# Attention with a token mixer: v instead of k times cos and sin, q transposed once, stacked k'v tiles, whole-tile stores and a new order

## The chip, the cores and the metric

One core of a Trainium2 chip. The metric is the device time of one execution in microseconds (us), compared as medians and as means over fast runs. A run counts as slow when it is more than 1.5% above the fastest run of the same kernel. Profiles show one execution; its span is about 1.8 us shorter than its time. The *granted clock* is the share of its full clock that TensorE was allowed. An *evacuation* is a copy of a result out of PSUM, the memory into which TensorE writes; a store has *landed* when its last byte has arrived.

## The reference, cut to what matters

```python
# q, k, v: (batch 8, heads 8, seq 576, dim 64) fp32; result (8, 576, 512) fp32
def phi(x, c, s):
    r = np.maximum(x, 0.0)
    return np.concatenate([r * c, r * s], axis=-1)      # 64 -> 128 features
q_p, k_p = phi(q, cos_w, sin_w), phi(k, cos_w, sin_w)   # angle = pi/2 * pos / 576
kv  = np.einsum('bhsf,bhsd->bhfd', k_p, v)
z   = np.sum(k_p, axis=2)
num = np.einsum('bhsf,bhfd->bhsd', q_p, kv)
den = np.einsum('bhsf,bhf->bhs', q_p, z)[..., None] + 1e-06
x   = num / den                                  # heads side by side: (8, 576, 512)
wq, wk = x @ w_q, x @ w_k                        # 512 -> 64
W_tok  = 1/8 * np.einsum('bsd,btd->bst', wq, wk)
out    = np.maximum(np.einsum('bst,btd->bsd', W_tok, x), 0.0) @ w_out
```

## The kernel before

The whole kernel is a list of words such as `MK.3.0@V`: an operation, its indices, and the engine (V VectorE, A ScalarE, G GpSimd, T TensorE with a PSUM bank, Y SyncE's DMA queue). Each engine executes its words in the order of the list. A *double pair* `H` is four heads of one batch. A *pair* `g` is two heads, which lie on the 128 partitions as 2 x 64 rows of 9 positions each. There are 16 double pairs and 32 pairs.

For each pair VectorE made two products of 1152 elements (`MK`: relu(k) times cos and sin; `EQ`: transposed q times cos and sin), one cast of k'v out of PSUM (`EK`), a denominator and its reciprocal (`RC`), and one normalisation (`XN`).

```python
def MK(eng, pb, H, s):                       # k' = relu(k) * (cos, sin), line L232
    eng.tensor_mul(kp[H % N_KP][:, lo:hi],
        rk[H % N_RK][:, lo:hi].unsqueeze(3).to_broadcast([P, n, C9, 2, D]),
        cossin.unsqueeze(1).to_broadcast([P, n, C9, 2, D]))

def DQ(eng, pb, H, s):                       # relu(q), written twice (QREP = 2)
    relu(eng, qd[H % N_QD][:, lo:hi]..., raw["q"]...to_broadcast([P, n * C9, QREP, D]))

def QK(eng, pb, g):                          # per pair: 18 products and 18 transposes
    for c in range(C9):
        for hh in range(2):
            p0 = hh * 64
            T.matmul(kvp[:, hh, :], kp[H % N_KP][p0:p0 + 64, i, c, :, :],       # L260
                     vb[H % N_VB][p0:p0 + 64, i, c, 0:D + 1], ...)
    ... # 18 transposes of the doubled q, 64 x 128 each (L269)

def NM(eng, pb, g):                          # 10 products over 128 rows, L292
    for hh in range(2):
        for u in range(SC):
            T.matmul(nv[:, hh, u, :], qpt[g % N_QPT][:, hh, 2 * u:2 * u + 2, :],
                     kvs[g % N_KV][:, hh, :], ...)

def RC(eng, pb, g):
    eng.tensor_scalar_add(rec[g % 4], den, EPS)
    eng.reciprocal(rec[g % 4], rec[g % 4])

# ... XT: 20 transposes of 64 rows per double pair; WQK, TK, KX, MX: the mixer

def WO(eng, pb, b, t):                       # one output tile: 4 products, L413
    for dmc in range(NDM):
        T.matmul(o, mix[...][:, dmc, base:base + P], wo_sb[:, dmc, :],
                 start=(dmc == 0), stop=(dmc == NDM - 1))

def ST(eng, pb, b, u, hi):                   # half a tile: 64 partitions
    dst = dataclasses.replace(out, offset=out.offset + row * DM,
        ap=[[C9 * DM, 64], [2 * DM, len(ts)], [1, DM]])
    eng.dma_start(dst, osb[n % N_OSB][64 * hi:64 * hi + 64, 0:len(ts), :])
```

Of the kernel before, what the change touches and what calls it, by code (L numbers as in the profile page):

```python
# [24 lines left out]
N_RAW, N_RK, N_KP, N_QD, N_VB, N_QPT, N_KV = 4, 2, 3, 3, 3, 4, 4  # L25
N_XS, N_XT, N_WQK, N_WKJ, N_KX, N_MIX, N_OSB = 3, 2, 2, 2, 2, 2, 6
QREP = 2
EPS_PE = False
LD_PAIR = True
SPLIT = (0, 1, 2, 3, 4, 5, 6, 7, 8, 9, 10, 11, 12, 13, 14, 15)  # L30
# [7 lines left out]
LD.k.1.0@Y LD.k.0.0@Y LD.v.0.0@Y LD.k.0.1@Y LD.q.1.1@Y LD.q.0.1@Y LD.q.0.0@Y LD.k.1.1@Y  # L38
LD.v.0.1@Y RK.1.0@V MK.1.0@V RK.0.0@V LD.v.1.1@Y LD.v.1.0@Y CV.0.0@V RK.0.1@A LD.q.2.1@Y
MK.0.0@V LD.q.1.0@Y MK.0.1@V LD.k.2.0@Y DQ.0.0@G LD.k.2.1@Y LD.v.2.1@Y RK.1.1@V DQ.0.1@G QK.0@T0  # L40
CV.0.1@A LD.v.2.0@Y EQ.0@V DQ.1.1@G QK.1@T2 CV.1.1@A LD.q.3.0@Y EK.0@V MK.1.1@V NM.0@T0 CV.1.0@A
LD.q.2.0@Y EQ.1@V QK.3@T4 DQ.2.1@G LD.v.3.0@Y RC.0@V EK.1@V LD.k.3.1@Y EQ.3@V DQ.1.0@G EK.3@V
LD.k.3.0@Y RK.2.0@A XN.0@V NM.3@T2 QK.2@T4 LD.v.3.1@Y RK.2.1@A MK.2.0@V MK.2.1@V CV.2.1@A
LD.k.4.0@Y RC.3@V QK.5@T0 CV.2.0@A LD.k.5.1@Y EQ.2@V NM.1@T6 EK.2@V DQ.3.0@G LD.q.3.1@Y XN.3@V
NM.2@T4 LW.qk@Y EK.5@V DQ.2.0@G RC.2@V RC.1@V LD.v.5.1@Y XN.2@V CV.3.0@G EQ.5@V LD.q.5.1@Y
XT.1@T2 XN.1@V LD.q.5.0@Y RK.3.0@A NM.5@T0 QK.4@T4 RK.3.1@A MK.3.0@V LD.k.5.0@Y XT.0@T6 CV.3.1@A
MK.3.1@V EX.1@A LD.v.4.0@Y EQ.4@V LD.q.4.0@Y EK.4@V RK.5.1@A RC.5@V QK.6@T2 LD.v.5.0@Y EX.0@A
NM.4@T4 EK.6@V CW.qk@G LD.q.4.1@Y RC.4@V RK.4.0@A MK.5.1@V WQK.0@T6 LD.k.4.1@Y CV.5.1@A DQ.3.1@G
XN.4@V LD.v.4.1@Y XN.5@V EW.0@A DQ.5.1@G LW.o@Y EQ.6@V DW.0@A XT.2@T0 TK.0@T4 LD.k.6.0@Y
MK.4.0@V QK.7@T6 EX.2@A QK.11@T2 EWK.0@V CV.4.0@G LD.k.6.1@Y EK.7@V EQ.7@V NM.6@T4 RK.5.0@G  # L50
LD.q.6.0@Y KX.0@T0 RC.6@V DQ.5.0@G XN.6@V NM.7@T6 LD.v.6.0@Y EKX.0@A CV.5.0@A DQ.4.0@G MX.0.2@T0
RC.7@V LD.k.7.0@Y MX.0.3@T4 EQ.11@V EMX.0.3@A EK.11@V LD.q.6.1@Y EMX.0.2@A MK.5.0@V MX.0.0@T4
MX.0.1@T2 RK.4.1@A QK.8@T0 LD.v.7.0@Y CV.4.1@G XN.7@V EMX.0.0@A DQ.4.1@G EQ.8@V EMX.0.1@A
XT.3@T6 QK.10@T4 EK.8@V EX.3@A MK.4.1@V NM.8@T0 EQ.10@V QK.9@T2 CW.o.0@G CW.o.1@A LD.v.6.1@Y
EK.10@V WQK.1@T6 EQ.9@V LD.q.7.0@Y RK.6.0@G EK.9@V NM.10@T4 RC.8@V LD.k.7.1@Y EW.1@A MK.6.0@V
WO.0.2@T2 LD.k.8.1@Y DQ.6.0@G RC.10@V NM.9@T6 XN.8@V EO.0.2@A WO.0.1@T3 LD.v.8.0@Y RK.6.1@A
XN.10@V CV.6.0@G TK.1@T2 EO.0.1@A LD.v.7.1@Y RK.7.0@G RC.9@V QK.12@T0 EWK.1@A XN.9@V DQ.6.1@G
LD.q.7.1@Y NM.11@T4 WO.0.0@T2 RC.11@V LD.k.8.0@Y MK.6.1@V KX.1@T3 EO.0.0@A LD.q.8.0@Y MK.7.0@V
DW.1@A WO.0.3@T6 CV.6.1@G EQ.12@V LD.k.9.0@Y EKX.1@A CV.7.0@A DQ.7.0@G MX.1.1@T2 EK.12@V
LD.v.10.0@Y XN.11@V EO.0.3@A QK.13@T0 EMX.1.1@A RK.7.1@G MX.1.0@T6 LD.k.9.1@Y QK.14@T4 EQ.13@V  # L60
EMX.1.0@A RK.8.1@G XT.4@T2 LD.v.8.1@Y EK.13@V EK.14@V MX.1.2@T6 MK.7.1@V WO.1.1@T0 EMX.1.2@A
LD.q.9.0@Y MK.8.1@V EX.4@A NM.12@T6 LD.q.8.1@Y WO.1.2@T1 DQ.7.1@G EQ.14@V EO.1.1@A LD.q.9.1@Y
RC.12@V XT.5@T2 CV.7.1@A RK.8.0@G XN.12@V NM.13@T4 LD.v.9.0@Y EX.5@A WO.1.0@T0 CV.8.0@G RC.13@V
DQ.8.0@G LD.k.10.1@Y XN.13@V MX.1.3@T6 RK.9.0@A QK.15@T2 LD.k.10.0@Y MK.8.0@V EO.1.2@A WQK.2@T4
EO.1.0@A MK.9.0@V LD.q.10.0@Y EMX.1.3@A CV.10.0@G EQ.15@V NM.14@T0 LD.v.9.1@Y EW.2@A QK.16@T6
RK.9.1@G RC.14@V CV.8.1@A EK.15@V LD.q.10.1@Y TK.2@T4 XN.14@V NM.15@T2 EWK.2@A WO.1.3@T5 DW.2@A
DQ.8.1@G LD.k.12.0@Y EQ.16@V EK.16@V LD.q.11.1@Y XT.6@T0 RC.15@V DQ.9.1@G QK.17@T6 EX.6@A
XN.15@V LD.k.11.1@Y KX.2@T4 CV.9.0@G EQ.17@V XT.7@T2 RK.10.1@G EKX.2@A EK.17@V EO.1.3@A EX.7@V
DQ.9.0@G MX.2.1@T0 NM.17@T6 EMX.2.1@A MX.2.0@T4 RC.17@V WQK.3@T2 EMX.2.0@A MK.9.1@V RK.10.0@A
CV.9.1@G XN.17@V MX.2.2@T0 QK.18@T4 EW.3@A LD.k.14.0@Y MK.10.1@V WO.1.4@T6 EMX.2.2@A ST.1.0.0@Y  # L70
MK.10.0@V LD.v.11.1@Y MX.2.3@T0 QK.19@T2 DW.3@G EQ.18@V ST.1.1.1@Y EMX.2.3@A TK.3@T7 DQ.10.0@G
EK.18@V ST.0.0.0@Y EK.19@V EWK.3@A NM.16@T0 EQ.19@V EO.1.4@A NM.18@T4 ST.1.0.1@Y WO.2.1@T7
DQ.10.1@G RC.16@V RC.18@V LD.k.11.0@Y XN.16@V QK.20@T2 ST.0.0.1@Y EO.2.1@A DQ.11.1@G XN.18@V
RK.12.0@A LD.v.10.1@Y KX.3@T0 RK.11.1@A CV.11.1@G LD.q.11.0@Y EQ.20@V NM.19@T4 EKX.3@A
LD.v.11.0@Y XT.8@T6 EK.20@V RC.19@V MX.3.1@T0 ST.0.1.0@Y EX.8@A MK.12.0@V WO.2.0@T2 LD.v.12.0@Y
XN.19@V RK.11.0@G WO.2.3@T3 LD.k.12.1@Y EMX.3.1@A MK.11.1@V ST.1.1.0@Y EO.2.0@A MX.3.2@T4
XT.9@T0 MK.11.0@V LD.v.12.1@Y QK.23@T6 EO.2.3@A LD.q.12.0@Y CV.10.1@G EX.9@V EMX.3.2@A NM.20@T2
ST.0.1.1@A DQ.11.0@G EK.23@V MX.3.3@T4 EQ.23@V WQK.4@T0 CV.11.0@A LD.q.13.1@Y RC.20@V EMX.3.3@A
LD.q.12.1@Y XN.20@V QK.22@T6 EW.4@A QK.21@T4 LD.k.13.0@Y EQ.22@V TK.4@T0 MX.3.0@T2 EK.21@V
RK.12.1@G ST.1.2.1@A WO.2.2@T1 EK.22@V EQ.21@V EWK.4@A LD.k.13.1@Y NM.23@T6 EMX.3.0@A MK.12.1@V  # L80
NM.22@T4 LD.v.13.1@Y EO.2.2@A KX.4@T0 RC.23@V RK.14.0@G CV.12.0@A XN.23@V NM.21@T2 ST.1.2.0@Y
DQ.12.0@G EKX.4@A WO.3.3@T1 RC.22@V LD.q.13.0@Y RC.21@V CV.12.1@G XN.22@V WO.3.0@T0 EO.3.3@A
LD.v.13.0@Y XN.21@V DW.4@A XT.11@T4 DQ.12.1@G ST.2.0.0@Y QK.24@T6 EX.11@V MX.4.2@T2 LD.q.14.0@Y
WO.3.2@T1 EMX.4.2@A EQ.24@V RK.13.0@G EO.3.0@A LD.v.14.0@Y EK.24@V MX.4.0@T2 MK.14.0@V QK.25@T4
EMX.4.0@A LD.k.15.0@Y MX.4.3@T6 RK.13.1@G WO.3.1@T0 EK.25@V EO.3.2@A EQ.25@V DQ.13.1@G
LD.k.14.1@Y EMX.4.3@V XT.10@T2 EO.3.1@A ST.2.0.1@Y MX.4.1@T4 WO.3.4@T1 MK.13.0@V EMX.4.1@A
ST.3.1.0@Y MK.13.1@V NM.24@T6 EO.3.4@A WO.4.0@T0 LD.v.15.0@Y CV.13.0@G RC.24@V EX.10@A XN.24@V
DQ.13.0@G NM.25@T4 LD.q.15.0@Y WO.4.1@T1 RC.25@V EO.4.0@A LD.k.15.1@Y CV.13.1@G XN.25@V QK.26@T2
EO.4.1@A DQ.14.0@G LD.q.14.1@Y QK.27@T6 CV.14.0@A EQ.26@V XT.12@T0 LD.v.14.1@Y RK.15.0@A
QK.28@T4 EK.26@V EK.27@V EX.12@A EQ.27@V RK.14.1@G ST.3.2.1@Y WQK.5@T2 EK.28@V LD.q.15.1@Y  # L90
MK.14.1@V WO.4.2@T6 EW.5@A MK.15.0@V ST.2.1.0@Y NM.27@T0 DW.5@G EQ.28@V EO.4.2@A NM.26@T2
TK.5@T7 CV.15.0@G RC.27@V EWK.5@A NM.28@T4 RC.26@V DQ.15.0@G WO.4.3@T6 XN.27@V RK.15.1@A RC.28@V
KX.5@T7 XN.26@V EO.4.3@A DQ.14.1@G QK.30@T0 EKX.5@A ST.4.1.1@Y XN.28@V MX.5.3@T2 MX.5.1@T6
LD.v.15.1@Y CV.14.1@G EQ.30@V EMX.5.3@A XT.13@T4 ST.4.1.0@Y EMX.5.1@A EK.30@V QK.29@T2 EX.13@V
ST.3.0.1@Y ST.2.1.1@A DQ.15.1@G MX.5.0@T0 NM.30@T6 EK.29@V ST.3.0.0@Y EMX.5.0@A EQ.29@V WQK.6@T4
ST.4.0.1@Y ST.3.1.1@A RC.30@V MK.15.1@V WO.5.0@T0 ST.3.2.0@Y EW.6@A XN.30@V CV.15.1@G ST.4.0.0@Y
NM.29@T2 DW.6@G TK.6@T1 RC.29@V MX.5.2@T4 QK.31@T6 EWK.6@V EMX.5.2@A XN.29@V KX.6@T1 EO.5.0@A
EK.31@V WO.5.4@T4 EQ.31@V ST.5.0.0@Y EKX.6@V NM.31@T2 ST.5.0.1@Y MX.6.0@T0 RC.31@V MX.6.1@T6
EMX.6.0@A WO.5.2@T5 XN.31@V EO.5.4@A EMX.6.1@V XT.14@T0 EO.5.2@A XT.15@T2 WO.5.3@T4 EX.14@V
EX.15@V WO.6.0@T5 EO.5.3@A WQK.7@T0 ST.5.2.0@A ST.5.2.1@Y EO.6.0@V WO.6.1@T2 EW.7@V MX.6.3@T4  # L100
DW.7@G MX.6.2@T0 EO.6.1@A TK.7@T3 EMX.6.2@V WO.5.1@T6 EWK.7@A ST.6.0.1@Y EMX.6.3@A ST.6.0.0@A
KX.7@T7 EO.5.1@V WO.6.3@T0 EKX.7@V ST.5.1.0@A ST.5.1.1@Y MX.7.1@T2 MX.7.3@T4 MX.7.0@T6 EMX.7.1@A
WO.6.2@T1 EMX.7.0@V EO.6.3@A EMX.7.3@V MX.7.2@T2 EO.6.2@A WO.7.1@T6 EMX.7.2@A ST.6.1.0@Y
WO.7.2@T7 ST.6.1.1@A EO.7.1@V WO.7.4@T0 EO.7.2@A WO.7.3@T1 ST.7.1.0@Y ST.7.1.1@A EO.7.4@V
WO.7.0@T2 ST.7.3.0@A EO.7.3@V ST.7.3.1@A ST.7.2.0@Y EO.7.0@A ST.7.2.1@Y ST.7.0.0@A ST.7.0.1@Y
"""


@with_exitstack
def kernel(  # L110
    ctx: ExitStack,
    tc: tile.TileContext,
    q: bass.AP,
    k: bass.AP,
    v: bass.AP,
# [83 lines left out]

    def part(H, s):  # L200
        return (s, s + 1) if H in SPLIT else (0, 2)

    def LD(eng, pb, t, H, s):
        lo, hi = part(H, s)
        b, h = divmod(H, 2)
# [48 lines left out]
    def QK(eng, pb, g):  # L254
# [8 lines left out]
        for c in range(C9):  # L263
            for hh in range(2):
                p0 = hh * 64
                src = qd[H % N_QD][p0:p0 + 64, i, c, :, :]
                if QREP == 1:
                    src = src.to_broadcast([64, 2, D])
# [240 lines left out]
```

## Time and profile before

The median was 130.89 us in three runs (130.32 to 133.51); the profiled run took 130.29 us, with a span of 128.5 us and a granted TensorE clock of 0.91.

The kernel has one long stage in which VectorE works almost without a break, and a tail in which TensorE finishes the mixer and the output product. The window view of the kernel before shows this, from the first cos/sin product on VectorE (4.1 us) to the last normalisation (108.6 us). Its columns are the stretch, its length, the busy time (with instruction counts) of PE, PEld, DVE, ACT and POOL, the granted clock, the DMA share and GB/s:

```profile
4.10:16.00 11.90, 7.07 (x128) 4.46 (x126) 8.47 (x16) 3.81 (x6) 6.12 (x5) 0.74 1.02 366
16.00:40.00 24.00, 19.15 (x519) 15.71 (x519) 21.99 (x48) 15.77 (x23) 15.45 (x16) 0.70 1.06 382
40.00:80.00 40.00, 36.09 (x848) 24.49 (x845) 37.86 (x80) 29.99 (x53) 26.32 (x28) 1.00 0.85 298
80.00:108.60 28.60, 26.85 (x587) 17.25 (x586) 27.51 (x62) 18.75 (x32) 18.42 (x21) 1.00 0.95 326
```

Subtract the DVE column from the length to get VectorE's idle time: 3.4, 2.0, 2.1 and 1.1 us; it is busy for 95.8 of the 104.5 us.

These further lines of the page of the kernel before are needed later: the chain that ended last, shared out by engine, the doubled q on GpSimd, and the half-tile stores.

```profile
DVE 31%; PE 30%; POOL 10%; DMA 8%; SPq 7%; issue 6%; ACT 3%; ACTq 2%; POOLq 0%
...
L195 POOL TENSOR_SCALAR qd<-qf 128x1152 bf16<-128x1152 f32 x32 | 39.1, 1231 | 12.7 <-DMA qf<-in_q_dram 11.6
...
out_dram<-osb SPq DMA_DIRECT2D x21, 256.0 KB, 4.4
out_dram<-osb ACTq DMA_DIRECT2D x9, 256.0 KB, 4.3
out_dram<-osb SPq DMA_DIRECT2D x9, 128.0 KB, 3.4
...
out_dram<-osb ACTq DMA_DIRECT2D x3, 128.0 KB, 4.0
```

The chain runs about equally through VectorE and TensorE, with 9% in the two queues that issue stores and loads (SPq, ACTq). There are 42 store issues, twelve of them on ScalarE's queue.

### The profile page before, as it was taken

How to read it: one execution, taken by the hardware profiler on the slowest of the kernel's cores; microseconds unless marked ns; L12 is line 12 of the kernel's file. 1: busy time of each engine (PE TensorE's matmuls, PEld its weight loads, DVE VectorE, ACT ScalarE, POOL GpSimd, SP SyncE). 2: the span in 40 equal slices, each digit the busy share in tenths (PEclk: the TensorE clock that was granted, in tenths of full speed). 3: DMA queues.
4: the chain of work that ended last, by engine and by line, in shares of the span. 5: the costliest groups of instructions: out<-in, count | busy, mean ns of one | idle time of the engine just before them, and what ended most of it. 6: DMA issues, size and time to landing. Idle time of an engine off the chain costs nothing.

```text
span 128.5 us, 5197 instructions
## 1 busy us (share of the span) xinstructions
PE 105.4 (82%) x2198; PEld 69.4 (54%) x2198; DVE 106.2 (83%) x227; ACT 77.5 (60%) x124; POOL 69.4 (54%) x81
## 2 busy tenths in 40 slices
PE   5935594887879979878999969889999999999900
PEld 2314584847667546566676557364576775543400
DVE  3466999987899999999999896999999998774600
ACT  7125443966396698974976758647977655147110
POOL 7009817098969979995078252389949740020000
PEclk9995558655799999999999999999999999999995
DMA  4999999999999999992068999999998799468793
GB/s 133 276 389 406 391 391 390 331 392 388 389 387 392 391 385 391 390 386 103 5 146 319 303 360 363 340 329 403 384 377 309 176 341 248 107 197 278 186 289 100
DMA packets 20711, 39.40 MB, mean 307 GB/s; under 512 B 3280, under 2 KB 3280, under 8 KB 20688
## 3 DMA queue, kind: packets, MB, share of 16 engines
q1 hardware_dynamic: 19152, 36.32, 81.8%
q10 hardware_dynamic: 1536, 2.75, 6.1%
q8 instruction: 17, 0.28, 0.9%
q14 instruction: 6, 0.05, 0.1%
HBM read 29.62 MB, written 9.44 MB: 304 GB/s over the span
## 4 chain that ended last, share of the span: by engine, by line
DVE 31%; PE 30%; POOL 10%; DMA 8%; SPq 7%; issue 6%; ACT 3%; ACTq 2%; POOLq 0%
DVE kp L232 10%; PE banks L413 10%; DVE xs L309 8%; DVE qpt L279 7%; POOL qd L195 5%; PE banks L260 5%; SPq L208 5%; DMA qf<-in_q_dram 5%; PE banks L269 4%; DMA vf<-in_v_dram 4%; PE banks L292 3%; SPq L430 2%; DVE rec L305 2%; PE banks L343 2%; POOL vb L189 2%
## 5 line engine op out<-in xcount | busy, mean ns | idle before, releaser
L195 POOL TENSOR_SCALAR qd<-qf 128x1152 bf16<-128x1152 f32 x32 | 39.1, 1231 | 12.7 <-DMA qf<-in_q_dram 11.6
L413 PE MATMUL banks<-wo_sb,mix 128*128 128x512 bf16 x144 | 36.0, 380 | 0.0
L232 DVE TENSOR_TENSOR kp<-rk,cossin 128x1152 bf16<-128x1152 bf16 x32 | 29.2, 932 | 1.4 <-POOL rk L195 1.3
L185 ACT COPY osb<-banks 128x512 f32<-128x512 f32 x31 | 18.0, 589 | 12.9 <-PE banks L413 8.2
L309 DVE TENSOR_TENSOR xs<-banks,rec 128x640 bf16<-128x640 f32 x32 | 25.4, 808 | 0.3
L279 DVE TENSOR_TENSOR qpt<-banks,cst 128x1152 bf16<-128x1152 bf16 x32 | 23.9, 746 | 1.1 <-PE banks L269 0.8
L401 ACT ACTIVATE mix<-banks 128x640 bf16<-128x640 f32 (+1 forms) x27 | 17.4, 656 | 8.7 <-PE banks L388 8.1
L260 PE MATMUL banks<-vb,kp 64*128 64x65 bf16 x576 | 16.7, 202 | 3.8 <-DVE kp L232 1.8
L413 PEld LDWEIGHTS <-mix 128*128 128x128 bf16 x144 | 12.1, 98 | 12.5 <-issue 1.4
L292 PE MATMUL banks<-kvs,qpt 128*128 128x65 bf16 x320 | 16.2, 203 | 3.1 <-DVE kvs L187 2.2
L269 PE MATMUL banks<-ident,qd 64*128 64x64 bf16 x576 | 16.2, 201 | 2.2 <-POOL qd L195 2.2
L292 PEld LDWEIGHTS <-qpt 128*128 128x128 bf16 x320 | 13.8, 103 | 7.1 <-DVE qpt L279 2.5
L260 PEld LDWEIGHTS <-kp 64*128 64x128 bf16 x576 | 13.6, 100 | 7.2 <-DVE kp L232 2.5
L193 ACT ACTIVATE rk<-kf 128x576 bf16<-128x576 f32 x15 | 10.1, 684 | 9.1 <-DMA kf<-in_k_dram 8.9
L195 POOL TENSOR_SCALAR rk<-kf 128x576 bf16<-128x576 f32 x14 | 11.3, 812 | 6.6 <-DMA kf<-in_k_dram 2.8
L189 POOL TENSOR_SCALAR vb<-vf 128x576 bf16<-128x576 f32 x17 | 12.3, 726 | 4.6 <-DMA vf<-in_v_dram 3.5
L269 PEld LDWEIGHTS <-qd 64*128 64x128 bf16 x576 | 12.9, 102 | 2.4 <-POOL qd L195 2.4
L185 ACT COPY xT<-banks 128x1280 bf16<-128x1280 bf16 x10 | 12.2, 1225 | 2.9 <-PE banks L326 2.9
L185 ACT CAST vb<-vf 128x576 bf16<-128x576 f32 x14 | 9.4, 673 | 4.7 <-DMA vf<-in_v_dram 4.5
L326 PE MATMUL banks<-ident,xs 64*128 64x64 bf16 x320 | 7.8, 196 | 4.2 <-DVE xs L309 4.1
L189 POOL TENSOR_SCALAR wq<-wqk 64x576 bf16<-64x576 bf16 x4 | 2.8, 712 | 14.9 <-DVE wqk L187 7.8
L343 PE MATMUL banks<-xT,wqk_sb 128*128 128x288 bf16 x64 | 10.1, 306 | 0.7 <-DVE xs L309 0.3
(46 smaller groups left out, 112.8 us busy)
## 6 DMA issues: line engine op xcount, KB each, us to landing
kf<-in_k_dram SPq DMA_DIRECT2D x32, 288.0 KB, 6.0
vf<-in_v_dram SPq DMA_DIRECT2D x32, 288.0 KB, 5.9
qf<-in_q_dram SPq DMA_DIRECT2D x32, 288.0 KB, 6.0
out_dram<-osb SPq DMA_DIRECT2D x21, 256.0 KB, 4.4
out_dram<-osb ACTq DMA_DIRECT2D x9, 256.0 KB, 4.3
out_dram<-osb SPq DMA_DIRECT2D x9, 128.0 KB, 3.4
wo_f<-in_moe_w_out_dram SPq DMA_DIRECT2D x1, 1024.0 KB, 8.3
out_dram<-osb ACTq DMA_DIRECT2D x3, 128.0 KB, 4.0
```

Source lines behind the costliest of these rows:

```text
L185: A.copy(dst, src)
L189: eng.tensor_scalar(dst, src, 1.0, 1.0, op0=ALU.mult, op1=ALU.mult)
L195: eng.tensor_scalar(dst, src, FMAX, 0.0, op0=ALU.min, op1=ALU.max)
L232: eng.tensor_mul(kp[H % N_KP][:, lo:hi], rk[H % N_RK][:, lo:hi].unsqueeze(3).to_broadcast([P, n, C9, 2, D]), cossin.unsqueeze(1).to_broadc ...
L260: T.matmul(kvp[:, hh, :], kp[H % N_KP][p0:p0 + 64, i, c, :, :], vb[H % N_VB][p0:p0 + 64, i, c, 0:D + 1], start=(c == 0), stop=(c == C9 - 1))
L269: T.transpose(qt[:, hh, c * D:(c + 1) * D], src, ident[p0:p0 + 64, p0:p0 + 64])
L279: eng.tensor_mul(qpt[g % N_QPT][:, :, 1:SLOTS, :], qk_views(at["QK", g])[0].rearrange("f h (c d) -> f h c d", c=C9), cst.unsqueeze(1).to_b ...
L292: T.matmul(nv[:, hh, u, :], qpt[g % N_QPT][:, hh, 2 * u:2 * u + 2, :], kvs[g % N_KV][:, hh, :], start=(u == 0), stop=(u == SC - 1 and not ...
L309: eng.tensor_tensor(xs[b % N_XS][:, :, 2 * pr:2 * pr + 2, :].rearrange("p u h d -> p h u d"), num_view(at["NM", g])[:, :, :, 0:D], rec[g % ...
L343: T.matmul(w[:, nh, :], wqk_sb[:, dmc, :], xT[b % N_XT][:, dmc, D + nh * HS:D + (nh + 1) * HS], start=(dmc == 0), stop=(dmc == NDM - 1))
L401: A.activation(dst, src, AF.Relu, scale=scale_moe)
L413: T.matmul(o, mix[b // 2 % N_MIX][:, dmc, base:base + P], wo_sb[:, dmc, :], start=(dmc == 0), stop=(dmc == NDM - 1))
```

## The change

The intent is to relieve VectorE, and to make the stores fewer and simpler.

- **k'v.** cos and sin go onto v, not k. The 64 features of relu(k) then stay 64, and the four heads of a double pair are stacked in 64x64 tiles of the array: 36 products of 131 columns per double pair (64 columns of v times cos, 64 of v times sin, the sums for the denominator).
- **q** is written once, transposed once per double pair for two heads at a time, and the cos/sin product reads the transposed copy twice.
- **k'v casts** become 16 larger ones, on ScalarE instead of VectorE. Most of VectorE's copies out of PSUM move to ScalarE too.
- **Stores.** The mixer is evaluated by halves of the tokens in natural row order, so an output tile is 128 rows in sequence: 21 issues of 128 partitions, all on SyncE, instead of 42 of 64 partitions.
- **x transposes** take all 128 rows: ten per double pair instead of twenty.
- **Order** is new throughout, and 26 constant products (`WU`) fill early gaps of TensorE.

The diff, cut to its core (the order lists, buffer declarations, the mixer's reordering and constants at the start are left out):

```diff
-N_RAW, N_RK, N_KP, N_QD, N_VB, N_QPT, N_KV = 4, 2, 3, 3, 3, 4, 4
+N_RAW, N_RK, N_VB, N_VV, N_QD, N_QPT, N_KV = 4, 2, 2, 3, 3, 4, 3
+XT_FULL = (0, 1, 2, 3, 4, 5, 6, 7, 8, 9, 10, 11, 12, 13, 14, 15)
 ...
-    def MK(eng, pb, H, s):
+    def VK(eng, pb, H, j):
         eng.tensor_mul(
-            kp[H % N_KP][:, lo:hi],
-            rk[H % N_RK][:, lo:hi].unsqueeze(3).to_broadcast([P, n, C9, 2, D]),
-            cossin.unsqueeze(1).to_broadcast([P, n, C9, 2, D]))
+            vv[H % N_VV][:, j, :, :, 0:D],
+            vb[H % N_VB][:, j].unsqueeze(2).to_broadcast([P, C9, 2, D]), cossin)
 ...
+    def KV(eng, pb, H):
+        for c in range(C9):
+            for j in range(2):
+                for r in range(2):
+                    T.matmul(kvp[64 * j:64 * j + 64, r, :], rk[H % N_RK][64 * r:64 * r + 64, j, c, :],
+                             vv[H % N_VV][64 * r:64 * r + 64, j, c]...[:, 0:NV], ...)
 ...
     def EQ(eng, pb, g):
+        qt = bank1(at["TQ", H] + r, 0, 2 * HC, BF16)...
+        eng.tensor_mul(qpt[g % N_QPT][:, :, 1:SLOTS, :],
+                       qt.unsqueeze(1).to_broadcast([P, 2, C9, D]), cst)
 ...
     def NM(eng, pb, g):          # 20 row-tiled products in place of 10
+        for u in range(SC):
+            for w in range(2):
+                for j in range(2):
+                    p0 = 64 * j
+                    T.matmul(nv[:, j, u, :], qpt[g % N_QPT][p0:p0 + 64, w, 2 * u:2 * u + 2, :],
+                             kvs[H % N_KV][p0:p0 + 64, r, w, 0:D + 1], ...)
 ...
-    def ST(eng, pb, b, u, hi):
+    def ST(eng, pb, b, u):
         dst = dataclasses.replace(
-            out, offset=out.offset + row * DM,
-            ap=[[C9 * DM, 64], [2 * DM, len(ts)], [1, DM]])
-        eng.dma_start(dst, osb[n % N_OSB][64 * hi:64 * hi + 64, 0:len(ts), :])
+            out, offset=out.offset + row * DM, ap=[[DM, P], [P * DM, len(ts)], [1, DM]])
+        eng.dma_start(dst, osb[n % N_OSB][:, 0:len(ts), :])
+
+    def WU(eng, pb, n):
+        for _ in range(n):
+            T.matmul(bank1(pb, 0, 2048, FP32), warm[:, 0:P], warm, start=True, stop=True)
```

## The prediction

> **What bounds the kernel now.** I read the page's busy shares first, then the 40 slices, then the groups, then time windows, and last the timeline of the end. VectorE is the busiest engine, and TensorE is near it:
>
> ```profile
> PE 105.4 (82%) x2198; PEld 69.4 (54%) x2198; DVE 106.2 (83%) x227; ACT 77.5 (60%) x124; POOL 69.4 (54%) x81
> ...
> DVE  3466999987899999999999896999999998774600
> ...
> PEclk9995558655799999999999999999999999999995
> DMA  4999999999999999992068999999998799468793
> ```
>
> The slices (3.2 us each) show three stages. Up to 16 us the engines wait for loads. From 16 to about 104 us VectorE is at nine tenths. After that it empties, and the windows show TensorE full instead (columns: stretch, its length, busy time with instruction counts by engine, clock, DMA share, GB/s):
>
> ```profile
> 48.00:56.00 8.00, 7.17 (x188) 4.91 (x181) 7.77 (x14) 7.11 (x11) 7.61 (x9) 1.00 1.05 389
> ...
> 104.00:112.00 8.00, 8.00 (x143) 4.98 (x142) 7.05 (x15) 3.33 (x6) 1.24 (x2) 1.00 0.75 218
> 112.00:120.00 8.00, 8.00 (x56) 3.48 (x54) 4.66 (x7) 4.04 (x8) 0.67 (x1) 1.00 0.71 214
> ```
>
> So the sum to make is: VectorE's queue up to its last normalisation (line L309), then TensorE's closing work, then one evacuation and one store. What VectorE does, by group:
>
> ```profile
> L232 DVE TENSOR_TENSOR kp<-rk,cossin 128x1152 bf16<-128x1152 bf16 x32 | 29.2, 932 | 1.4 <-POOL rk L195 1.3
> L309 DVE TENSOR_TENSOR xs<-banks,rec 128x640 bf16<-128x640 f32 x32 | 25.4, 808 | 0.3
> L279 DVE TENSOR_TENSOR qpt<-banks,cst 128x1152 bf16<-128x1152 bf16 x32 | 23.9, 746 | 1.1 <-PE banks L269 0.8
> ...
> L187 DVE CAST kvs<-banks 128x130 bf16<-128x130 f32 x32 | 8.7, 281 | 1.1 <-ACT xT L185 1.0
> ```
>
> The timeline's last normalisation on VectorE starts at 107.79 us and takes 0.82, so it ends at 108.6. The end of the run:
>
> ```profile
> 117.71 4.49 PE L413 MATMUL banks<-wo_sb,mix 128*128 128x512 bf16 x20
> ...
> 120.26 3.15 ACTq L430 DMA_DIRECT2D out_dram<-osb  x3
> ...
> 123.51 0.58 ACT L185 COPY osb<-banks 128x512 f32<-128x512 f32 x1 [3.28 <-issue]
> ```
>
> TensorE is done at 122.2. The last evacuation sits behind three store issues on ScalarE's own queue and ends only at 124.1; the last store lands at 128.5. Split: 108.6 to the last normalisation, 13.6 of TensorE, 1.9 to the last evacuation's end, 4.4 for the store.
>
> **What the Trainium skill says.** "VectorE: DVE Perf Modes", section "The perf-mode tier table", with its section on why tensor_tensor has no 4x mode: two results a cycle at 0.96 GHz is the ceiling for bf16. 1152/1.92 is 600 ns, and the trace's uncontended product takes 752 (median), so 150 fixed; it agrees. The change's products keep 1152 elements with unit innermost step, so I expect no other speed. "SBUF — State Buffer", section "Who interferes with whom": a VectorE instruction with two SBUF inputs contends with a GpSimd instruction that reads SBUF. L232 has two and spreads from 696 to 1692 ns; L279, with one operand in PSUM, stays within 696 to 759. It agrees. "TensorEngine Tiling (Array Packing)", section "Restrictions and Gotchas": column tiling excludes the fast weight load. The 64-column weight loads of L371 average 112 ns against 98 for the 128-column ones of L326, so a load of half the columns is not cheaper here. "TensorE: Matmul & The Clock Gate", section "What's actually happening": after an idle window of some 3.4 us the clock halves. The slices' clock of 0.5 to 0.8 between 10 and 35 us agrees.
>
> **The change, part by part.** I counted the operations in both orders by engine.
>
> *VectorE.* The cos/sin product moves from k to v (32 of the same shape, line for line the same cost, 29.2). The q product reads one transposed copy twice but still writes 1152 elements: 23.9. Normalisation 25.4 and the two small denominators 4.9 + 6.9 stay. Gone to others: 32 casts of k'v (8.7), three relus of k and one cast of v (1.7 + 0.8), three of six xT copies (2.4), four of five mix and all five output evacuations (2.9 + 3.5), one wqk and two kx (1.6); one small copy comes (0.3). Adding the groups gives 116.8 before against 95.3 after. The first is 106.2 as busy time, since neighbours overlap by some 9%; so 87 after. Most of the saving that counts is what lay before 108.6 us. VectorE was busy 97 us up to there; after, 95.3 less tail copies (1.9) and the initial fills (0.9) is 92.5, times 0.91 is 84.
>
> *ScalarE.* It gains 16 k'v casts (0.37 each by the similar 256-element cast, 5.9), 14 q relus (9.6), three xT copies (3.7), four mix, five output, one wqk and two kx evacuations (2.7 + 2.9 + 0.6 + 0.7), a table of double size (0.5). It loses eight relus of k, two casts of v, three wq copies and one wkj (5.5 + 1.3 + 2.0 + 0.4) and all store issues. Net +17.4 on a summed 83.2, some 101 summed, 94 us busy at the same overlap of 7%.
>
> *GpSimd.* q is written once: 18 pieces of 576 at about 0.67 instead of 32 of 1.23. With 25 relus of k, 20 casts of v, seven wq copies, the weights and the start's fills: 12 + 19.5 + 14.5 + 5 + 1.8 + 4, 57 us against 69.
>
> *TensorE, warm.* Transposes of q halve: 18 take 0.26, so 16 groups fewer save 4.2. k'v becomes 36 products of 131 columns in 64x64 tiles per double pair instead of two groups of 18 (0.28 each). If four tiles run at once the streams are 9 x 131/2.4, 0.49 us; if weight loads serialise it nears 1.0. I take 0.8 (an estimate between the two): 12.8 against 9.0, +3.8. The numerators double in number at half the rows, and 18 row-tiled products of 65 columns take 0.28, so 20 take 0.31, as the ten now do. Full transposes: ten of 128 columns, an estimated 0.55 against 0.35, +3.2. Sum: about +3 on an estimated 84 (the group times at full clock), off the path until the tail. The 26 constant products cost 0.2 to 0.43 each in gaps and should keep the clock up from 8 to 35 us, where VectorE lost 4 us in waits and several links on the chain were TensorE groups at half speed (0.68 against 0.28 for the k part).
>
> *Stores.* Same bytes, 21 whole-tile issues on SyncE in place of 42, twelve of which were on ScalarE. The last evacuation no longer waits for issues.
>
> *The sum.* Start: the first four loads landed at 3.6, 4.8, 6.6 and 7.3 us before. The first product on v needs loads 1 and 4 and a cast of 0.67 first, so it starts near 8 instead of 4.1, with about 3 us of idle until the first transposed q (its second half is load 7, landed at 9.5). VectorE then ends its normalisations at 8 + 84 + 3 + idle in the middle. From 16 to 108 us it idled 5.1; I keep 6, as ScalarE is fuller: about 101 to 102. TensorE's work after the last normalisation in the new order: 12 output tiles x 0.9, two full transposes 1.1, seven mix products 1.1, 1.0 + 0.1 + 0.7: 14.8. Then 0.6 evacuation and 4.7 store. 101.7 + 14.8 + 5.3 is a span of 121.8. The profiled run's time was 1.8 above its span and the median of the timed runs is 0.6 above it; so 124.2.
>
> **The rivals.** (1) ScalarE becomes the bound. For it: 94 us busy beside VectorE's 87, and the k'v casts, xT and mix evacuations that TensorE waits for are all in its queue. Against it: of these some 12 are tail and 4 start, leaving 78 in a stretch of 97 (80%). If its waits reach VectorE, I would expect 3 to 5 us more: 128. (2) DMA becomes the bound. 39.4 MB at the 390 GB/s of the middle slices is 101 us. VectorE will need a double pair (1.77 MB, 4.5 us of DMA) about every 5.3 us instead of 6, so the loads stay barely ahead in the first half; starting 4 us later than before it could eat the gain: 126 to 128. Against it: before, DMA stood nearly still from 57 to 64 us and still cost VectorE hardly more than 1.5 us. (3) The 64x64 tiles don't run side by side and a k'v group costs 1.5 to 2 us. TensorE would then be full from 90 us on and the time 127 to 129. (4) The contention on L232 (180 ns above the median each, 5.8 us in all) falls with GpSimd's load: up to 3 us less, 121.
>
> **Range and chances.** Zero idle in the middle gives 118, and rival (4) with it about 117; two rivals together undo the gain. I take 124.2, with 119.8 to 128.6 to hold it 8 times in 10. 2% faster is below 128.3: chance 0.81. Within 2%: 0.16. Slower by over 2%: 0.03, since no engine's sum comes near 130.
>
> **What would show it right or wrong.** Right: VectorE's busy time near 87, no VectorE casts of k'v, last normalisation near 102, clock at 1.0 by about 20 us, ScalarE busy near 94, TensorE full after the last normalisation for about 15 us, and 5 to 6 us from its end to the end. Wrong: VectorE idling on ScalarE or TensorE in the middle for over 10 us; a k'v group over 1.2 us; products on v slower than 932 ns for their padded rows; waits for loads in the middle.

## The result

The changed kernel takes 123.75 us in the median of four runs (123.41 to 125.56), against 130.92 for the kernel before in the same rounds: the ratio is 0.947, with a 95% interval of 0.941 to 0.953. A ratio here is the mean time of one kernel's fast runs over that of the other's in the same rounds, so it is not quite the ratio of the medians quoted.

The first profile of the changed kernel fell on its slowest run (125.56 us). This is the granted clock on that page, in 40 slices:

```profile
PEclk9995999999855999999999999999999999999999
```

The clock was halved between about 33 and 40 us. That this made the run slow is not shown: its mean clock was 0.959, and another of the four runs had 0.958 and took 123.47 us. For the comparison with the kernel before, whose profiled run was fast, I therefore ran the changed kernel again unaltered and read that profile (122.67 us, fast). Its own clock is in the page below.

> The changed kernel, not altered, for a profile in the fast state and for the spread of its times. Both theories: 123.4 to 124.1 us. The first profile fell in a run of 125.56 us with the clock halved for 6.8 us around 34 to 40 us and the last normalisation at 106.15 us. If that stretch made it slow, a fast profile has a span near 122 and the last normalisation near 104.3, with the same 14 us of TensorE and 3.7 us of evacuation and store behind it. Rival: the end is what varies, and the last normalisation stays at 106.

The six runs of the repeat had a median of 123.82 us (122.67 to 125.96; before in the same rounds 132.27), ratio 0.943 (0.935 to 0.952), in line with the first result. The fast profile ended its last normalisation at 103.2 us, 3 us earlier than the slow one, and had the same tail. The lines of its page that answer to those of before:

```profile
PE 106.1 (88%) x2096; PEld 63.9 (53%) x2096; DVE 86.7 (72%) x174; ACT 91.5 (76%) x155; POOL 57.8 (48%) x90
...
DVE  2026499899799998999999996977897789412000
...
PEclk9998699999999999999999999999999999999998
...
PE 51%; DVE 23%; issue 7%; ACT 5%; DMA 5%; POOL 4%; SPq 2%; ACTq 0%; POOLq 0%
...
L219 DVE TENSOR_TENSOR vv<-vb,cossin 128x1152 bf16<-128x1152 bf16 x32 | 27.1, 873 | 7.2 <-ACT vb L180 6.4
L257 DVE TENSOR_TENSOR qpt<-banks,cst 128x1152 bf16<-128x1152 bf16 x32 | 22.9, 748 | 5.7 <-PE banks L250 5.3
L292 DVE TENSOR_TENSOR xs<-banks,rec 128x640 bf16<-128x640 f32 x32 | 25.2, 810 | 0.5
...
L190 POOL TENSOR_SCALAR qd<-qf 128x576 bf16<-128x576 f32 x18 | 14.1, 783 | 14.8 <-DMA qf<-in_q_dram 14.3
...
out_dram<-osb SPq DMA_DIRECT2D x15, 512.0 KB, 5.4
out_dram<-osb SPq DMA_DIRECT2D x6, 256.0 KB, 2.5
```

VectorE's busy time fell from 106.2 to 86.7 us, with the three large groups almost unchanged in number and duration. ScalarE rose from 77.5 to 91.5. TensorE stayed at 106, and the chain moved over to it: 51% of the span instead of 30%, while the two store and load queues fell from 9% to 2%. GpSimd, which now writes 18 pieces of q once instead of 32 twice (14.1 us instead of 39.1), fell from 10% to 4%. The same windows of this run, cut at its own first product on v (8.22 us) and its own last normalisation (103.2 us):

```profile
8.22:16.00 7.78, 5.49 (x98) 2.46 (x100) 5.08 (x8) 3.30 (x6) 2.13 (x4) 0.78 1.05 400
16.00:40.00 24.00, 20.40 (x554) 13.88 (x548) 22.11 (x44) 16.98 (x29) 16.75 (x22) 1.00 1.06 381
40.00:80.00 40.00, 38.47 (x862) 24.58 (x855) 37.55 (x74) 35.55 (x63) 25.48 (x34) 1.00 0.94 336
80.00:103.20 23.20, 23.20 (x499) 14.81 (x498) 19.12 (x41) 18.15 (x34) 9.24 (x14) 1.00 0.92 348
103.20:120.90 17.70, 14.00 (x98) 6.50 (x94) 1.98 (x4) 12.08 (x22) 0.67 (x1) 0.98 0.55 207
```

VectorE's idle time is now 2.7, 1.9, 2.5 and 4.1 us. The new thing is the fourth line: from 80 to 103.2 us TensorE is busy for 23.20 us of 23.20, and VectorE, which was the full one there before, rests for 4.1 us. (Ends of matmuls are modelled, so a full TensorE is one that always has an instruction at work, not one at its peak.)

The timeline of the end of this run:

```profile
111.85 5.35 PE L403 MATMUL banks<-wo_sb,mix 128*128 128x512 bf16 x24
...
117.24 0.59 ACT L180 COPY osb<-banks 128x512 f32<-128x512 f32 x1 [0.23 <-PE banks L403]
```

TensorE ends at 117.2, the last evacuation follows at once and ends at 117.8, and the last store has landed at 120.9. Term by term, in us:

| Term | before | after, fast profile | moved |
|---|---|---|---|
| first cos/sin product on VectorE | 4.1 | 8.2 | +4.1 |
| VectorE busy to the last normalisation | 95.8 | 83.9 | -11.9 |
| VectorE idle in that stretch | 8.7 | 11.1 | +2.4 |
| last normalisation ends | 108.6 | 103.2 | -5.4 |
| TensorE after it | 13.6 | 14.0 | +0.4 |
| to the end of the last evacuation | 1.9 | 0.6 | -1.3 |
| to the last landing | 4.4 | 3.1 | -1.3 |
| span | 128.5 | 120.9 | -7.6 |

So 5.4 us came from the long stage and 2.6 from the end, less 0.4 of tail.

### The profile page after: what moved, and what is told of

The parts are those of the page before. It is cut to its first block, busy times and chain, and to the rows that moved or that the text cites. A ratio compares the mean times of both kernels' runs of the same rounds, so it can differ in the third digit from the quotient of the medians.

```text
span 123.8 us, 4941 instructions
## 1 busy us (share of the span) xinstructions
PE 106.9 (86%) x2077; PEld 65.6 (53%) x2096; DVE 88.2 (71%) x174; ACT 91.8 (74%) x155; POOL 57.8 (47%) x90
## 4 chain that ended last, share of the span: by engine, by line
PE 54%; DVE 19%; issue 9%; ACT 5%; DMA 4%; POOL 4%; SPq 2%; POOLq 0%; ACTq 0%
PE banks L403 22%; DVE xs L292 6%; PE banks L236 5%; PE banks L332 5%; PE banks L310 5%; DVE qpt L257 5%; DVE vv L219 5%; DMA qf<-in_q_dram 4%; PE banks L271 4%; PE banks L379 4%; PE banks L250 3%; PE banks L422 3%; PE banks L360 3%; DVE rec L287 2%; SPq L197 2%
## 5 line engine op out<-in xcount | busy, mean ns | idle before, releaser
L219 DVE TENSOR_TENSOR vv<-vb,cossin 128x1152 bf16<-128x1152 bf16 x32 | 28.9, 927 | 5.6 <-ACT vb L180 5.6
L391 ACT ACTIVATE mix<-banks 128x576 bf16<-128x576 f32 x31 | 19.6, 659 | 2.9 <-PE banks L379 1.9
L190 POOL TENSOR_SCALAR qd<-qf 128x576 bf16<-128x576 f32 x18 | 13.3, 743 | 15.2 <-DMA qf<-in_q_dram 13.7
L184 POOL TENSOR_SCALAR vb<-vf 128x576 bf16<-128x576 f32 x20 | 14.8, 742 | 6.1 <-DMA vf<-in_v_dram 2.9
L271 PE MATMUL banks<-kvs,qpt 64*128 64x65 bf16 x640 | 14.3, 192 | 0.1
L271 PEld LDWEIGHTS <-qpt 64*128 64x128 bf16 x640 | 12.0, 95 | 4.1 <-issue 2.4
L236 PE MATMUL banks<-vv,rk 64*64 64x131 bf16 x576 | 12.6, 229 | 1.0 <-DVE rec L287 0.5
L310 PE MATMUL banks<-ident,xs 128*128 128x128 bf16 x160 | 11.5, 220 | 1.2 <-issue 0.8
L236 PEld LDWEIGHTS <-rk 64*64 64x64 bf16 x576 | 9.9, 112 | 4.6 <-issue 2.1
L310 PEld LDWEIGHTS <-xs 128*128 128x128 bf16 x160 | 9.5, 98 | 3.6 <-issue 1.2
L188 ACT ACTIVATE qd<-qf 128x576 bf16<-128x576 f32 x14 | 9.6, 687 | 1.8 <-DMA qf<-in_q_dram 1.8
```

Source lines behind the costliest of these rows:

```text
L184: eng.tensor_scalar(dst, src, 1.0, 1.0, op0=ALU.mult, op1=ALU.mult)
L190: eng.tensor_scalar(dst, src, FMAX, 0.0, op0=ALU.min, op1=ALU.max)
L219: eng.tensor_mul(vv[H % N_VV][:, j, :, :, 0:D], vb[H % N_VB][:, j].unsqueeze(2).to_broadcast([P, C9, 2, D]), cossin)
L236: T.matmul(kvp[64 * j:64 * j + 64, r, :], rk[H % N_RK][64 * r:64 * r + 64, j, c, :], vv[H % N_VV][64 * r:64 * r + 64, j, c].rearrange("p w ...
L271: T.matmul(nv[:, j, u, :], qpt[g % N_QPT][p0:p0 + 64, w, 2 * u:2 * u + 2, :], kvs[H % N_KV][p0:p0 + 64, r, w, 0:D + 1], start=(u == 0 and ...
L310: T.transpose(xv[:, i, u, :], x, ident)
```

## The experiments

Twelve kernels ran, the repeat above among them. Each had runs of the kernel before; values are compared by their ratios to it. The theory at the start was that the gain is VectorE's relief plus the simpler end. The rivals were that the clock (the constant products) or TensorE's shorter work made it, and that ScalarE or the loads now limit the changed kernel.

### The constant products

```diff
-... TQ.1@T0 WU.5@T2 EQ.2@V ... TQ.0@T2 WU.2@T4 EQ.0@V ...
+... TQ.1@T0 EQ.2@V ... TQ.0@T2 EQ.0@V ...      (all WU words out of the order)
```

> The 26 constant products are taken out of the changed kernel, nothing else. Theory: without them the clock is at half between about 10 and 33 us as in the kernel before (20.5 us at half against 10.2), the TensorE groups between VectorE's steps take longer, and the time rises by 1 to 3 us (124.7 to 127). Rival: TensorE is not what VectorE waits for that early, or the products themselves delay the transposes behind them by as much (five of them stand 2.3 us before the second transposed q), and the time stays within 0.6 us of the unaltered kernel.

Median 123.66 us (123.28 to 124.72), ratio 0.946 (0.939 to 0.953); the repeat 0.943. The clock did sink in the profiled run; this is its line on the page of this kernel:

```profile
PEclk9997555599996799999999999999999999999999
```

The mean clock of the profiled runs went from 0.983 to 0.931, with half rate from about 11 to 24 us and again from 38 to 41; over all six runs of each it was 0.966 and 0.950 in the mean. The time moved by 0.3%, inside the intervals. The rival was right: the constant products raise the clock somewhat, and this gives no time that can be measured. TensorE had room in those first stretches (20.4 of 24 us busy with the constant products in).

### Whole or half transposes of x

```diff
-XT_FULL = (0, 1, 2, ..., 15)
+XT_FULL = ()
```

> Transposes of the normalised tile by halves (20 of 64 columns in row tiles) in place of 10 full ones, in the changed kernel. A full group takes 0.56 us in the profile and a group of halves took 0.35 in the kernel before: TensorE loses 16 x 0.21 = 3.4 us of work, 0.4 of it after the last normalisation. Theory that TensorE is now a bound from 80 us on: 0.8 to 2 us less (121.8 to 123). Rival, VectorE bounds up to its last normalisation and TensorE only in the tail: 0.4 us less at most (123.2 to 124).

Median 127.0 us (125.21 to 128.91), ratio 0.965 (0.955 to 0.976): 2.3% slower than the repeat, against both theories. Ten transposes of 128 rows were expected to be dearer than twenty of 64. This is the chain of the repeat, the whole transposes (columns: start, duration, what):

```profile
102.98 1.12 PE banks L310 x20
104.10 0.86 PE banks L403 x4
```

and this the chain of the kernel with half transposes:

```profile
82.01 0.40 PE banks L314 x20
82.41 0.97 PE banks L403 x4
```

Ten whole transposes take 0.56 us (20 in 1.12), twenty halves 0.40. But the four output products that follow take 0.97 us after half transposes and 0.86 after whole ones. In the repeat's chain from 100 us on, too, each group of four takes 0.86 us after work on the whole array and 0.97 after row- or column-tiled work. Together 1.37 against 1.42, so the saving of 0.16 shrinks to 0.05. Why the kernel got slower by over 2% is not settled. Its chain runs through loads for 40% of the span, against 5% in the repeat, but no run tells whether that is a cause. In its profiled run (the fastest of the six) the clock was 0.86 from 16 to 40 us instead of 1.00, and VectorE did 20.4 us of work there instead of 22.1; but runs of the two kernels with nearly the same mean clock (0.956 in the repeat, 124.08 us; 0.959 here, 126.99 us) still differ by 3 us.

### VectorE's small work: the denominators

Both kernels, with the addition of the epsilon left out (the padding rows of q set to 1 so that no denominator is zero; the result is still correct):

```diff
-            eng.tensor_scalar_add(rec[g % 4], den, EPS)
-            eng.reciprocal(rec[g % 4], rec[g % 4])
+            eng.reciprocal(rec[g % 4], den)
 ...
-        V.memset(t[:, :, 0, :], 0.0)
+        V.memset(t[:, :, 0, :], 1.0)
```

> The addition of 1e-6 to the denominators is left out and the reciprocal reads PSUM directly (the padding of q is set to 1 so that no denominator is 0); results differ by some 1e-6 relative. VectorE loses 32 instructions of 0.15 us, 4.8 us summed and about 6 with their issue gaps. If VectorE is still the bound up to the last normalisation: 4 to 6 us less (117.7 to 119.7). If TensorE has become the bound in the second half, as the chain (54% TensorE, 19% VectorE) suggests: 1 to 2.5 us less (121.2 to 122.7).

After: median 123.83 us (121.66 to 125.69). Only two of six runs were fast; their mean of 122.4 is 1.0 below that of the repeat's four fast runs (123.4), within the theory of 1 to 2.5 us, but the medians are equal. VectorE's busy time fell by 3.9 us to 82.8, and the last normalisation ended at 103.3 as in the repeat. The windows of this kernel:

```profile
40.00:80.00 40.00, 37.15 (x822) 23.84 (x821) 34.53 (x57) 33.73 (x61) 25.43 (x34) 1.00 0.97 345
80.00:103.20 23.20, 23.20 (x494) 14.61 (x493) 18.68 (x33) 18.14 (x34) 10.14 (x13) 1.00 0.89 333
```

and one of its waits over the whole run, in us in total, times, longest:

```profile
DVE rec L286 <- PE banks L271: 4.6, 8, 2.1
```

The 3.9 us that VectorE saved became waiting for the numerators (L271) on TensorE, a wait that is not among those listed for the repeat. Most of it, 3.5 us, lies between 40 and 80 us, where TensorE is busy for 37.15 of 40 us; from 80 us on TensorE is full as before. After the change, VectorE's work alone no longer sets the time; the theory of 4 to 6 us fell.

> The kernel before, with the addition of 1e-6 left out and the reciprocal reading PSUM, the same edit that changed nothing in the changed kernel. VectorE loses 4.9 us summed. If VectorE bounded the kernel before up to its last normalisation, as the prediction says: 3 to 5 us less (ratio 0.962 to 0.977). Rival: before, too, the time was set by loads and TensorE and VectorE was only busy beside them: under 1.3 us less (ratio over 0.99).

Before: median 129.98 us (127.99 to 136.13) against 132.55, ratio 0.973 (0.963 to 0.983) from two fast runs; over all runs the ratio of the means is 0.985. The last normalisation ended at 106.3 instead of 108.6. The same relief helped the kernel before by 1.5 to 2.7%, and the changed one by 0.2% (all runs) to 0.8% (fast runs). With two fast runs on either side the contrast is likely, not sure; it fits an engine that was the bound and is now one of several near-equal bounds.

### The k'v casts

In the kernel before, all 32 casts from VectorE to ScalarE (`EK.g@V` becomes `EK.g@A`); in the kernel after, the 16 from ScalarE back to VectorE (`EK.H@A` becomes `EK.H@V`).

> The kernel before, with the 32 casts of k'v moved from VectorE (8.7 us) to ScalarE (32 x 0.28 = 9 us) in the places where they stood. If relief of VectorE alone is the gain: 3 to 6 us less. Rival: in ScalarE's queue the casts wait behind copies of 0.6 to 1.2 us, the numerators that need them come later, and the move gives under 2 us or costs time.

> The changed kernel with its 16 casts of k'v moved back from ScalarE to VectorE (16 x about 0.42 = 6.7 us more on VectorE, 6.1 less on ScalarE). VectorE was 86.7 us busy, with 13 us of waits up to its last normalisation. If those waits are slack that TensorE sets, since 4 us less VectorE work gave nothing: 0 to 1.5 us more. If VectorE and TensorE are both near the bound: 2.5 to 5 us more.

Before: median 132.02 us (129.88 to 134.41), ratio 0.990 (0.979 to 1.001), unclear: some 1%, at most 2.1. In its profile, VectorE waited 5.3 us for numerators on TensorE and 2.7 for casts on ScalarE instead of working on the casts itself. After: median 125.15 us (122.69 to 127.28) with one fast run; VectorE's busy time was 91.0 us. The median is 1.3 us above the repeat's, the one fast run 0.7 below the mean of the repeat's fast runs, so a cost is not shown. As far as these runs can tell, which engine casts k'v is worth 2% at most, and the gain cannot be put down to this part of VectorE's relief.

### The stores

In the kernel before, the twelve stores on ScalarE's queue moved to SyncE (`ST.b.u.hi@A` becomes `ST.b.u.hi@Y`), half tiles as they were.

> The kernel before, with its twelve ScalarE store issues moved to SyncE and nothing else. Theory: the 3.28 us that the last evacuation waited for store issues on ScalarE's queue goes; it comes straight after the last output product, so 1.5 to 2.2 us less (ratio 0.983 to 0.989). Rival: the wait moves to SyncE, whose six last issues took 9.4 us for the queue's pace, and the last store lands no sooner: within 0.6 us.

Median 131.41 us (130.75 to 133.09) against 132.55, ratio 0.997 (0.990 to 1.003): the theory failed. The last evacuation did move, from 124.1 to 123.5, but the stores now queued behind each other. SyncE's timeline of this kernel:

```profile
118.92 8.02 SPq L430 DMA_DIRECT2D out_dram<-osb  x10
```

Ten issues take 8.02 us, to 126.9, 3.4 us after the last evacuation; the end is at 129.8. The wait moved from ScalarE to SyncE.

In the kernel after, each whole-tile store was issued as two of 64 partitions, all still on SyncE:

```diff
-        eng.dma_start(dst, osb[n % N_OSB][:, 0:len(ts), :])
+        for lo in (0, 64):
+            dst = ...  offset=out.offset + (row + lo) * DM, ap=[[DM, 64], [P * DM, len(ts)], [1, DM]]
+            eng.dma_start(dst, osb[n % N_OSB][lo:lo + 64, 0:len(ts), :])
```

> The changed kernel with each whole-tile store issued as two stores of 64 partitions, as many issues (42) as the kernel before, all on SyncE. Bytes and order stay. If the pace of issues on one queue is what delayed the last store in the kernel before with all its stores on SyncE (10 issues in 8.0 us, the last one 3.4 us after its data were ready): 1.5 to 2.5 us more. Rival, the stores' bytes or the evacuations set the end: within 0.6 us.

Median 128.88 us (126.66 to 132.34) against 132.46, ratio 0.967 (0.960 to 0.974), so 2.5% slower than the repeat's 0.943. SyncE's queue in the timeline of this kernel, and its last evacuation:

```profile
117.83 5.81 SPq L420 DMA_DIRECT2D out_dram<-osb  x8
...
119.81 0.58 ACT L180 COPY osb<-banks 128x512 f32<-128x512 f32 x1 [0.23 <-PE banks L403]
```

The last evacuation ends at 120.4, but SyncE issues until 123.6, and the end is at 126.5: 6.1 us after the evacuation instead of 3.1. The eight issues follow each other without a break, one every 0.73 us. In the unaltered kernel SyncE's last issue looks like this:

```profile
117.85 0.33 SPq L418 DMA_DIRECT2D out_dram<-osb  x1
```

A whole-tile issue takes 0.33 us there, with twice the bytes. Like for like, the median is 0.39 us over its 21 issues against 0.61 over the 42 of the split kernel, and 0.61 on SyncE in the kernel before. So the shape and the number of the stores are worth about 3 us; this is the largest part of the gain that one experiment isolates. Not all of it need lie at the end. The last normalisation of this profile also came 2.6 us later (105.8 us against 103.2), and SyncE's queue makes up 7% of its chain against 2%, most of that in load issues: loads share this queue with the stores. How the cost divides was not separated. Why an issue of 64 partitions is slower than one of 128 is open.

### TensorE's work

The output product of batches 0 to 3 sums two of its four parts (some 7.6 us of TensorE's work, 36 products of 0.21). Its output is wrong, which doesn't matter for the time.

```diff
-        for dmc in range(NDM):
+        nd = 2 if b < 4 else NDM
+        for dmc in range(nd):
             T.matmul(o, mix[...], wo_sb[:, dmc, :],
-                     start=(dmc == 0), stop=(dmc == NDM - 1))
+                     start=(dmc == 0), stop=(dmc == nd - 1))
```

> Wrong results on purpose. In the changed kernel the output products of batches 0 to 3 sum two of their four parts: 18 tiles lose 0.43 us each, 7.7 us of TensorE work, all of it before the last normalisation. If TensorE bounds the changed kernel from about 40 us on, so that 5 us of VectorE work more or less changed nothing: 4 to 7 us less (117 to 120). Rival, the bound is the chain of short waits between engines and not TensorE's sum: under 2 us less.

After: median 123.53 us (121.28 to 126.7), ratio 0.924 (0.916 to 0.931) from two fast runs of mean 121.7. Against the repeat's ratio that is 2%, some 2.6 us: less than the 4 to 7 us that a TensorE bound would give, and a little more than the rival's 2. The window from 40 to 80 us of its profile, a slow run of 123.6 us:

```profile
40.00:80.00 40.00, 32.98 (x850) 22.57 (x846) 37.67 (x71) 34.91 (x63) 23.91 (x33) 1.00 0.91 322
```

TensorE has 7 us free here, and VectorE is as full as in the repeat (37.67 against 37.55). VectorE had no room to use them.

> The same edit, wrong on purpose, in the kernel before: 7.7 us of TensorE work less before the last normalisation. Theory that VectorE bounded the kernel before up to there: under 2 us less (ratio over 0.985), where 4.9 us of VectorE work gave 1.6 to 2.7%. Rival, both kernels are bound by TensorE's sum: 4 to 7 us less (ratio 0.947 to 0.97).

Before: median 136.54 us (132.17 to 139.03) against 132.46, ratio 1.006 (0.998 to 1.014) from three fast runs: the same. The clock of this kernel's profile (a slow run):

```profile
PEclk9985559555999999999999955999999999999995
```

Here the clock halved once more, from about 78 to 84 us. The three fast runs, too, had a mean clock of 0.90, against 0.92 for the fast runs of the kernel before. So taking work from TensorE did not help the kernel before; whether the lower clock took back a part of the relief, these runs cannot separate.

### The loads

In the kernel after, only the first four double pairs are loaded and their buffers reused. Its output is wrong, which doesn't matter for the time.

```diff
     def LD(eng, pb, t, H, j):
+        if H >= N_RAW:
+            return
```

> Wrong results on purpose. In the changed kernel the loads of q, k and v stop after the first four double pairs (7 MB); the later ones work on what lies in the buffers, so there is no load to wait for from about 25 us on. Theory: loads pace the first 40 us, where TensorE has idle time and constant products between useful work, and TensorE's sum the rest: 3 to 6 us less (118 to 121), with TensorE full from about 25 us on. Rival, loads run ahead of use throughout: within 1 us. If the loads bound the whole middle: over 8 us less.

Median 122.25 us (121.63 to 122.69), ratio 0.927 (0.923 to 0.932). All loads after the first quarter are worth about 1.7% against the repeat's ratio, less than the 3 to 6 us of the theory that loads limit the new order. All six runs are fast and lie within 1.1 us, where the repeat spreads over 3.3: in this comparison most of the spread from run to run goes away with the loads.

## Why the prediction was right, point by point

- **The time.** Predicted 124.2 us, measured 123.75; range 119.8 to 128.6. That it is so close is partly luck, as the terms below show.
- **VectorE's work** was right: 84 us predicted to the last normalisation, 83.9 measured; 87 in all, 86.7 measured. The first product on v was expected near 8 and came at 8.22. The products on v cost no more for their padded rows (873 ns in the mean, against 932 on k; over all profiles 855 to 927 against 916 to 949).
- **Idle in the middle** is the term that was mis-sized. The prediction kept 3 us at the start and 6 from 16 us on; measured were 2.7 and 8.4. The step behind it was "off the path until the tail" for TensorE's work. Going by the windows, it held to 80 us. From 80 us TensorE is full, and VectorE's idle time there went from 1.1 to 4.1 us, 3.0 more. The waits of VectorE between 80 and 103.2 us, in the repeat, name TensorE first (VectorE's copies of transposed x, 1.7 of the 4.1 us):

```profile
DVE xT L182 <- PE banks L310: 1.7, 2, 1.1
```

  The last normalisation came at 103.2 instead of 101.7. (The prediction's own terms, 8 + 84 + 3 + 6, add up to 101; it wrote 101 to 102 and carried 101.7 on.) That TensorE is full there is shown by the window; that a shorter TensorE queue in just that stretch would bring the normalisation forward was not run, since the half-length output product relieved the batches before it.
- **The tail** was 0.8 shorter than predicted (14.0 against 14.8), and evacuation and store 1.6 shorter (3.7 against 5.3). The prediction gave the last store 4.7, near the 4.4 of the half tile before; the whole tile at the end landed after 3.1. These two misses offset the first: the span of 121.8 predicted is 120.9 in the fast profile. And the median lay 1.2 above the profiled run's time, where 0.6 was predicted. So the total is closer than its terms by luck.
- **The mechanism of the end** was only half seen. The prediction said that evacuations would no longer wait for store issues on ScalarE. Moving those issues alone gained nothing (131.41 against 132.55 us, ratio 0.997). The whole tiles are what makes SyncE keep up.
- **The constant products** were given the clock and, with caution, some of the start. They raised the clock and gave no time that can be measured. The rule that the prediction cites for the clock, an idle window of some 3.4 us, is not what the trace of the kernel before shows: before the half rate from 9.8 us on, TensorE was busy for 1.13 of 3.41 us, and before that from 23.5 us on for 1.75 of 3.42. An empty window was not needed.
- **TensorE's groups** came out as estimated or a little better: k'v 0.65 us (0.8), transposes of q 0.26 (0.26), numerators 0.31 (0.31), whole transposes 0.56 (0.55).
- **Rival 1 (ScalarE)**: busy 91.5 us (94 predicted), and 35.6 of 40 in the middle; moving its casts away gained nothing measurable. It is near the bound; nothing shows it to be the bound. **Rival 2 (loads)**: about 1.7%. **Rival 3**: its cause did not occur (0.65 us), yet its sign, a full TensorE late in the run, did, from 80 us. **Rival 4**: the product on v is 59 ns shorter than that on k was in the two fast profiles, 1.9 us in all, of the 3 it allowed; over all profiles the two ranges given above overlap.

What stays open: VectorE, TensorE and ScalarE are now close to each other. Relieving VectorE alone (the denominators) or TensorE alone (half the output product) gave about 2% or less; both at once was not run. Of the 7.6 us between the two profiles, the experiments isolate some 3, the stores. The rest came with the moved copies, q written once (and GpSimd's relief with it) and the new order together. The casts had no measurable share; the others were not undone one by one, and what each is worth is not shown. No run gives a correct kernel that is clearly faster than the changed one.

## What to carry to other kernels

When two engines are nearly full, relief of one pays only up to the other: before the change, 4 us less of VectorE's small work gave about 2%, after it 1% or less, which the spread of the runs does not resolve. Look at the windows of the last third and not only at the busy sums, for a second engine may be full just there. Count and shape the stores as carefully as the work: with halves of a tile the queue that issues them was still busy 3 us after the last result was ready.

## What the Trainium skill lacked or had wrong

- "DMA: Bandwidth & Descriptors", section "Issuing engines are not separate DMA queues", says that the time to initiate a DMA is usually small relative to the DMA. For a single store that holds here: the last 14 issues of 64 partitions took 0.60 us of the queue and 3.2 us to the landing (medians). But eight in a row kept the queue busy for 5.81 us, 3.2 us past the last evacuation, and the kernel was about 3 us slower. Issues of 128 partitions with twice the bytes took 0.37 (median of the last seven of the repeat). I found no page that states the issue time by shape.
- "TensorEngine Tiling (Array Packing)", section "Key Properties", says that a change of tiling mode drains TensorE, without a figure. Here four output products took 0.97 us after row-tiled work and 0.86 after whole-array work, 0.11 more, and that took back most of what half transposes save (0.16 us).
- "VectorE: DVE Perf Modes", section "The perf-mode tier table", lists tensor_tensor with any PSUM operand at one result a cycle. Here 1152 bf16 elements with one operand in PSUM took 746 and 748 ns in the mean, as long as the uncontended product with both operands in SBUF (752, median). For a bf16 operand in PSUM the table's entry does not hold; the page's own later section "Why PSUM operands drop a tier" allows more for bf16. For fp32 (640 elements in 810 ns) it agrees.
